# A decode layer on one core: K0 ahead of the q weights, wo behind V15, spread batch rows with one output store, and a W_down tail in rows 6, 2, 1

## The chip, the cores and the metric

The kernel runs on 1 core of one Trainium2 chip. The metric is the device time of one execution in microseconds (us), median of several executions. One execution was recorded by the hardware profiler; the durations below come from that one. Engines: PE (matmul), PEld (PE's weight loads), DVE (vector), ACT (scalar), POOL (GpSimd), SP (sync, which issues nearly all the loads).

## What is computed

One token for each of 4 sequences, through attention over a window of the cache and a gated FFN, all in bf16:

```python
def _A_ref(x, k_cache, v_cache, wq, wo):      # x: 4 x 1 x 576
    W = min(4096, max(256, Sk // 4))          # Sk = 16384, so W = 4096
    q = (x @ wq).reshape(B, Sq, 32, 128)...
    k = jnp.repeat(k_cache[:, :, Sk - W:, :], 2, axis=1)   # 16 key heads, 32 query heads
    v = jnp.repeat(v_cache[:, :, Sk - W:, :], 2, axis=1)
    p = _softmax(einsum("bhqd,bhkd->bhqk", q, k) * 128 ** -0.5)
    return einsum("bhqk,bhkd->bhqd", p, v)... @ wo
h = x + _A_ref(_layernorm(x), ...)
gate, up = h_norm @ W_gate, h_norm @ W_up     # 576 x 4608 each; h_norm = _layernorm(h)
h2 = h + ((gate * (gate > 0)) * up) @ W_down  # 4608 x 576
```

So 4 x 16 x 4096 x 128 keys and as many values (67 MB each), and four weight matrices of 4.7 or 5.3 MB, are read once; the arithmetic on them is small.

## The kernel before, in words

**Loads.** SP issues the loads in the order written in the code, one queue, and waits in that order: a load whose place in SBUF is still being read holds up all that come after it. `place` (line 220) keeps for each block of the arena who reads it last, and makes a new load there wait for that reader. `add_kv` (239) loads a tile of 4.19 MB, four key heads of one sequence: K0 to K15 and V0 to V15, into a ring of four slots. The order is wq (4.19 MB, and 0.52 MB more into the buffer pT), K0 to K4, V0, K5, V1, K6, ... K15, V11, V12, V13, V14, wo, V15, then W_gate, W_up, and W_down in four chunks, the last of them in rows 0 to 6 and 6 to 9. With this order wq has slot 3 and K0, K1, K2 have slots 0, 1, 2; K3 takes slot 3 again, K4 slot 0. The weights wo, W_gate, W_up and W_down lie where the q matrices and the four slots were.

**Attention.** A tile K is turned in place by two DVE transposes (`turn_k`, line 420, halves w = 0 and 1; the transpose itself is line 428), then PE multiplies it with q (`pe_qk`, 431; its matmul is line 446): 16 matmuls per half, four per head. `by_head` (31) names the halves that are turned in a second layout, in which PE reads the keys with another stride: in the profile the transpose takes about 7.3 us instead of 4.4, a matmul 0.227 us instead of 0.43 at full clock. Before the change these are the second halves of K0, K2, K3 and K4. Scores of four tiles (one sequence) gather in PSUM; `row_max` (451), `head_max` (456) and `exps` (464) make the exponentials, eight ACT operations; `turn_p` (477) turns them with two DVE transposes; `pe_pv` (483) multiplies with V; `select_o`, `weights` and `finish_o` reduce to the output of a sequence. `do_k` and `do_v` (561, 587) write the order out by hand. For g = 4 the row max, one head of QK(4,0), the head max and the exponentials of sequence 0 come ahead of the transpose of K4's second half.

**Start.** POOL builds constants (291 to 339), among them a memset of 6.9 us over the q area (299). ACT loads x (348), DVE takes its statistics (350) and normalizes; PE turns x (`pe_x`), DVE stores it (`dve_x`, 396 to 402); then c_am and c_msk, two DVE operations on a POOL constant (538, 540). `pe_q` (379) multiplies with wq, ACT evicts (`act_q`), 32 small matmuls turn q (QT), DVE stores it (`dve_q`, "qkeep", line 405), ACT spreads it into the block matrices (`put_q`, 412, "QW").

**End.** WO (622), layer norm by matmuls with ones, the FFN (GU, 668, gate first, then up), its product (HH, 675), transposes (681), DOWN (701): 144 matmuls of 144 columns, four column groups n in four partition groups of 32. DVE evicts [128, 144] (704). The four batch rows lie in partitions 32n to 32n+3, and four stores write them, two from SP and two from ACT (706 to 708).

Of the kernel before, what the change touches and what calls it, by code (L numbers as in the profile page):

```python
# [11 lines left out]
B = 4  # L12
D = 576
# [17 lines left out]
def by_head(g, w):  # L31
    return (g, w) in ((0, 1), (2, 1), (3, 1), (4, 1))

# [87 lines left out]
def bass_sequential_preLN__sliding_block_cached__glu_gated_reglu__decode_kernel(  # L121
# [12 lines left out]
    with ExitStack() as es:  # L134
        cnt = [0]

        def sb(name, shape, dt):
            return es.enter_context(nc.sbuf_tensor("sb_" + name, shape, dt))
# [54 lines left out]
        tmp5 = sb("tmp5", [128, DC, B], FP32)  # L193
        out_sb = sb("out_sb", [128, 144], BF16)


# [36 lines left out]
        def ring_slot():  # L233
            s = ring[0] % NSLOT
            ring[0] += 1
            return s
# [15 lines left out]
        def last_rows(W):  # L252
            return W[512:576, :].rearrange("r (a n) -> (r a) n", a=2)

        s = ring_slot()
        wq_off = slot0 + s * TILE
        place(("wq", 0), wq_off, TILE, "QMM",
              lambda e: e.dma_start(out=arena[:, wq_off:wq_off + TILE], in_=main_rows(A_wq)), key=f"slot{s}")
        P.dma("sync", ("L", "wq", 1), lambda e: e.dma_start(out=pT[:, 0:2048], in_=last_rows(A_wq)), "d_wq1")
        for g in range(NTILE):  # L260
            add_kv("K", g)
            if g >= 4:
                add_kv("V", g - 4)
# [3 lines left out]
        for g in range(NTILE - 4, NTILE):  # L267
            if g == NTILE - 1:
                place(("wo",), WO_OFF, H * D, "WO",
                      lambda e: e.dma_start(out=arena[:, WO_OFF:WO_OFF + H * D], in_=A_wo.rearrange("(p r) n -> p (r n)", p=128)))  # L270
            add_kv("V", g)
        gu_off = {}
        off = WO_OFF + H * D
# [20 lines left out]

        pool("c_xnT", lambda e: e.memset(xnT[:, :, :], 0.0))
        pool("c_m40", lambda e: e.memset(c_m4[:, :, :], 0.0))
# [3 lines left out]
        pool("c_idf0", lambda e: e.memset(ident_f[:, :], 0.0))  # L300
        pool("c_idf", lambda e: e.affine_select(out=ident_f[:, :], in_=ident_f[:, :], pattern=[[-1, 128]],
                                                compare_op=ALU.not_equal, fill=1.0, base=0, channel_multiplier=1), ["c_idf0"])
        pool("c_am0", lambda e: e.memset(c_am[:, :, :, :], 0.0))
# [39 lines left out]
        dve("c_par", lambda e: e.tensor_scalar(out=par[:, 1:2], in0=par[:, 0:1], scalar1=-1.0, scalar2=1.0,  # L343
                                               op0=ALU.mult, op1=ALU.add), ["c_par0"])


# [17 lines left out]
        def chunk(t, td, c):  # L364
            return td if c == 4 else t[:, 0:512].rearrange("b (p r) -> b r p", r=4)[:, c, :]
# [161 lines left out]
        def finish_o(b):  # L527
# [9 lines left out]
        dve_x()  # L537
        dve("c_am", lambda e: e.tensor_reduce(out=am[:, :], in_=c_am[:, :, :, :].rearrange("p a m s -> p a (m s)"), axis=AX.X, op=ALU.max),
            ["c_am1"])
        dve("c_msk", lambda e: e.tensor_scalar(out=msk[:, :], in0=am[:, :], scalar1=-1.0, scalar2=BIG, op0=ALU.add, op1=ALU.mult), ["c_am"])  # L540
        pe_q()
# [5 lines left out]
        dve("c_e8", lambda e: e.tensor_reduce(out=e8[:, :], in_=c_e8[:, :, :], axis=AX.X, op=ALU.max), ["c_e81"])  # L547
        dve("c_sel", lambda e: e.tensor_reduce(out=sel4[:, 0:4], in_=c_s4[:, :, :], axis=AX.X, op=ALU.max),
            ["c_s41", "c_sel0"])
        for q in range(4):  # L550
            dve("c_selc", lambda e, q=q: e.tensor_copy(out=selc[:, q, :, q], in_=e8[:, :]), ["c_e8", "c_selc0"])
        turn_k(0, 0)
        turn_k(0, 1)

        late = []

        def flush():
            while late:
                late.pop(0)()

        def do_k(g):
            b, qd = divmod(g, 4)
            if g:
                turn_k(g, 0)
            if g == 5:
                turn_p(0, 0)
                turn_p(0, 1)
            flush()
            if g == 4:
                row_max(0)  # L570
                pe_qk(g, 0, range(1))
                head_max(0)
                exps(0)
                turn_k(g, 1)
                pe_qk(g, 0, range(1, 4))
                put_q(2)
            else:
                if g:
                    turn_k(g, 1)
# [50 lines left out]
        for c in range(DC):  # L630
            pe("HT", lambda e, c=c: e.matmul(m_ps[:, c * 4:(c + 1) * 4], lhsT=chunk(part, partd, c), rhs=sel4[:, 0:4],
                                             start=True, stop=True), ["part0", "part1", "partd", "c_sel"] if c == 0 else [])
# [18 lines left out]
        dve("n2a", lambda e: e.tensor_tensor(out=tmp5[:, :, :], in0=tmp5[:, :, :], in1=rstd_bc, op=ALU.mult), ["n1", "s6"])  # L651
        dve("n2", lambda e: e.tensor_copy(out=hnT[:, 0:4, 0:4], in_=tmp5[:, 0:4, :]), ["n2a", "c_hnT"])
        for a in range(2):
            dve("n3", lambda e, a=a: e.tensor_scalar(out=hnT[:, 4 + a, 0:4], in0=tmp5[:, 4, :], scalar1=par[:, a:a + 1], scalar2=None,
                                                     op0=ALU.mult), ["n2a", "c_hnT"])
# [32 lines left out]
        for n in range(4):  # L688
            pe(None, lambda e, n=n: e.matmul(bank[0][32 * n:32 * n + 32, 0:144], lhsT=sel4[:, :], rhs=part[:, 144 * n:144 * (n + 1)],
                                             start=True, stop=False, skip_group_check=True), [("G", 0)])  # L690
        for n in range(4):
            pe(None, lambda e, n=n: e.matmul(bank[0][32 * n:32 * n + 32, 0:144], lhsT=ident_b[0:B, 0:32], rhs=x_bf[:, 144 * n:144 * (n + 1)],
                                             start=False, stop=False, skip_group_check=True))
        for j in range(4):
            wv = arena[:, wd_off[j]:wd_off[j] + WDJ].rearrange("p (r n) -> p r n", n=D)
            for r in range(9):
                for n in range(4):
                    deps = []
                    if n == 0 and (r == 0 or (j == 3 and r == 6)):
                        deps = [("L", "wd", j, r)] + (["HC0", "HC1", "HC2"] if j == 0 else [])  # L700
                    pe("DOWN", lambda e, j=j, r=r, n=n, wv=wv: e.matmul(  # L701
                        bank[0][32 * n:32 * n + 32, 0:144], lhsT=hhT[:, r * 128 + 32 * j:r * 128 + 32 * j + 32],
                        rhs=wv[:, r, 144 * n:144 * (n + 1)], start=False, stop=(j == 3 and r == 8), skip_group_check=True), deps)
        dve("OUT", lambda e: e.tensor_copy(out=out_sb[:, :], in_=bank[0][:, 0:144]), ["DOWN"])
        orow = out.rearrange("b s d -> (b s) d")
        for n in range(4):
            P.dma("sync" if n % 2 == 0 else "scalar", ("O", n),
                  lambda e, n=n: e.dma_start(out=orow[:, 144 * n:144 * (n + 1)], in_=out_sb[32 * n:32 * n + 4, :]), f"d_out{n}", ["OUT"])
        P.op("sync", None, None, [("O", n) for n in range(4)])
        P.emit(nc, es)  # L710
# [28 lines left out]
```

## Time and profile before

| | us |
|---|---|
| median of 3 runs | 383.94 (383.39 to 384.01) |
| the profiled execution, its own time | 384.01 |
| its span (first to last event on the core) | 382.2 |
| PE, DVE, ACT, POOL busy | 281.2, 222.0, 37.5, 16.1 |
| bytes moved in the span | 159.81 MB, mean 418 GB/s |
| queue of SP's loads, share of the 16 DMA engines' span | 97.5% |
| transposes of K (line 428), 32 | 152.8 in all |
| matmuls with K (line 446), 512 | 212.6 in all |

The page's slices show the rates along the span, each slice 9.55 us; a digit is a share in tenths, PEclk the clock granted to PE:

```profile
PEclk9967999987999897898998987989998956558667
DMA  8999999998999999999999999999999999999993
GB/s 330 439 439 434 429 429 429 422 434 336 432 424 415 433 439 435 432 436 434 425 425 429 434 439 432 427 429 436 425 430 436 439 427 433 421 450 422 420 406 143
```

Busy times overlap, so they don't add up to the span. In rows of the timeline the columns are start, busy time, engine, line, operation, out<-in, count, and in brackets the idle time ahead of it and who ended it. SPq is SP issuing a load.

### The profile page before, as it was taken

How to read it: one execution, taken by the hardware profiler on the slowest of the kernel's cores; microseconds unless marked ns; L12 is line 12 of the kernel's file. 1: busy time of each engine (PE TensorE's matmuls, PEld its weight loads, DVE VectorE, ACT ScalarE, POOL GpSimd, SP SyncE). 2: the span in 40 equal slices, each digit the busy share in tenths (PEclk: the TensorE clock that was granted, in tenths of full speed). 3: DMA queues.
4: the chain of work that ended last, by engine and by line, in shares of the span. 5: the costliest groups of instructions: out<-in, count | busy, mean ns of one | idle time of the engine just before them, and what ended most of it. 6: DMA issues, size and time to landing. Idle time of an engine off the chain costs nothing.

```text
span 382.2 us, 3671 instructions
## 1 busy us (share of the span) xinstructions
PE 281.2 (74%) x1629; PEld 92.1 (24%) x1629; DVE 222.0 (58%) x157; ACT 37.5 (10%) x95; POOL 16.1 (4%) x38
## 2 busy tenths in 40 slices
PE   0509999969989792979996948889969537036654
PEld 0202223313222221322221212222212213015322
DVE  4159999789484918965737369766464455102111
ACT  3120000070000006100000041000000340000100
POOL 8700000000000000000000000000000000000000
PEclk9967999987999897898998987989998956558667
DMA  8999999998999999999999999999999999999993
GB/s 330 439 439 434 429 429 429 422 434 336 432 424 415 433 439 435 432 436 434 425 425 429 434 439 432 427 429 436 425 430 436 439 427 433 421 450 422 420 406 143
DMA packets 6390, 159.81 MB, mean 418 GB/s; under 512 B 740, under 2 KB 744, under 8 KB 1384
## 3 DMA queue, kind: packets, MB, share of 16 engines
q1 hardware_dynamic: 6352, 159.59, 97.5%
q8 instruction: 12, 0.20, 0.2%
q14 instruction: 2, 0.02, 0.0%
q10 hardware_dynamic: 24, 0.01, 0.0%
HBM read 159.58 MB, written 0.00 MB: 418 GB/s over the span
## 4 chain that ended last, share of the span: by engine, by line
PE 47%; DMA 34%; DVE 15%; ACT 2%; SPq 1%; issue 1%
PE psb L446 40%; DMA sb_arena<-in_A_k_cache_dram 19%; DVE sb_arena L428 12%; DMA sb_arena<-in_B_W_down_dram 9%; DMA sb_arena<-in_A_v_cache_dram 7%; PE psb L493 5%; ACT sb_pp L471 2%; DVE sb_o_sel L505 1%; DVE sb_o_tmp L501 1%; DVE sb_pp L480 1%; PE psb L465 0%; PE psb L530 0%; SPq L285 0%; DVE sb_gm L459 0%; DVE sb_gm L461 0%
## 5 line engine op out<-in xcount | busy, mean ns | idle before, releaser
L446 PE MATMUL psb<-sb_arena 128*128 128x512 bf16 x512 | 212.6, 585 | 22.2 <-DVE sb_arena L428 22.1
L428 DVE STREAM_TRANSPOSE sb_arena<-sb_arena 128x4096 f32<-128x4096 f32 x32 | 152.8, 4804 | 48.0 <-DMA sb_arena<-in_A_k_cache_dram 48.0
L446 PEld LDWEIGHTS psb<-sb_arena 128*128 128x128 bf16 x512 | 56.6, 113 | 169.6 <-issue 134.9
L493 PE MATMUL psb<-sb_arena,sb_pp 128*32 128x512 bf16 x512 | 36.0, 433 | 22.5 <-DMA sb_arena<-in_A_v_cache_dram 15.9
L471 ACT ACTIVATE sb_pp<-psb,sb_stat 128x512 bf16<-128x512 f32 x32 | 24.9, 845 | 259.6 <-DVE sb_stat L466 259.6
L501 DVE TENSOR_TENSOR sb_o_tmp<-psb,sb_qm 128x512 f32<-128x512 f32 x16 | 10.8, 676 | 27.0 <-PE psb L493 26.9
L493 PEld LDWEIGHTS psb<-sb_arena,sb_pp 128*32 128x32 bf16 x512 | 13.6, 106 | 47.6 <-issue 23.0
L453 DVE TENSOR_REDUCE sb_stat<-psb 128x1 f32<-128x1024 f32 x4 | 4.9, 1224 | 26.7 <-PE psb L446 26.7
L480 DVE STREAM_TRANSPOSE sb_pp<-sb_pp 128x2048 bf16<-128x2048 bf16 x8 | 18.0, 2278 | 1.4 <-ACT sb_pp L471 1.4
L505 DVE TENSOR_REDUCE sb_o_sel<-sb_o_tmp 128x128 f32<-128x512 f32 x16 | 16.6, 1036 | 0.5
L530 PE MATMUL psb<-sb_o_sel,sb_selw 128*32 128x32 f32 x128 | 2.2, 221 | 16.3 <-DVE sb_o_sel L505 16.3
L668 PE MATMUL psb<-sb_arena,sb_hnT 128*32 128x384 bf16 x120 | 9.0, 483 | 6.6 <-DMA sb_arena<-in_B_W_up_dram 4.5
L675 DVE TENSOR_TENSOR sb_pp<-psb,sb_pp 128x384 bf16<-128x384 f32 x3 | 1.5, 551 | 13.7 <-PE psb L668 13.7
L371 PE MATMUL psb<-sb_ident_b,sb_xn_bf 4*128 4x4 bf16 x4 | 0.3, 174 | 9.9 <-DVE sb_xnd_bf L360 9.9
L668 PEld LDWEIGHTS psb<-sb_arena,sb_hnT 128*32 128x32 bf16 x120 | 4.4, 135 | 10.6 <-DMA sb_arena<-in_B_W_up_dram 4.9
L299 POOL MEMSET sb_arena<- 128x8192 f32 x1 | 6.9, 6925 | 0.0
L513 PE MATMUL psb<-sb_stat,sb_sameh 128*128 128x1 f32 x8 | 1.7, 286 | 6.7 <-DVE sb_stat L511 6.7
L471 ACT ACTIVATION_READ_ACCUMULATOR sb_pp<-psb,sb_stat 128x1 f32 x32 | 6.5, 204 | 0.0
L530 PEld LDWEIGHTS psb<-sb_o_sel,sb_selw 128*32 128x32 f32 x128 | 1.7, 132 | 17.4 <-DVE sb_o_sel L505 17.4
L701 PE MATMUL psb<-sb_arena,sb_pp 128*32 128x144 bf16 x144 | 3.8, 249 | 2.6 <-DMA sb_arena<-in_B_W_down_dram 2.1
L384 PE MATMUL psb<-sb_arena,sb_xnT 128*32 128x512 bf16 x32 | 3.2, 573 | 2.8 <-DMA sb_arena<-in_A_wq_dram 2.8
L414 ACT COPY sb_arena<-sb_q_keep 32x128 bf16<-32x128 bf16 x16 | 4.8, 302 | 1.5 <-DVE sb_q_keep L405 1.4
(123 smaller groups left out, 71.4 us busy)
## 6 DMA issues: line engine op xcount, KB each, us to landing
sb_arena<-in_A_k_cache_dram SPq DMA_DIRECT2D x16, 4096.0 KB, 19.7
sb_arena<-in_A_v_cache_dram SPq DMA_DIRECT2D x16, 4096.0 KB, 24.4
sb_arena<-in_A_wo_dram SPq DMA_DIRECT2D x1, 4608.0 KB, 15.6
sb_arena<-in_B_W_gate_dram SPq DMA_DIRECT2D x1, 4608.0 KB, 30.5
sb_arena<-in_B_W_up_dram SPq DMA_DIRECT2D x1, 4608.0 KB, 41.9
sb_arena<-in_A_wq_dram SPq DMA_DIRECT2D x1, 4096.0 KB, 12.3
sb_arena<-in_B_W_down_dram SPq DMA_DIRECT2D x3, 1296.0 KB, 31.3
sb_arena<-in_B_W_down_dram SPq DMA_DIRECT2D x1, 864.0 KB, 32.9
```

Of the source, the lines that this page charges most:

```text
L299: pool("c_qW", lambda e: e.memset(arena[:, 0:2 * QWW].bitcast(FP32), 0.0))
L414: act(("QW", b), lambda e, i=i: e.copy(out=bass.AP(tensor=arena, offset=32 * i * AW + b % 2 * QWW + 32 * i, ap=[[AW, 32], [128, 4], [514, ...
L428: dve(("TRA", g, w), lambda e: e.transpose(out=dst, in_=src), [("L", "K", g)] if w == 0 else [])
L446: pe(("QK", g, w), lambda e, off=off, steps=steps, wo_=wo_, qd=qd, first=first, last=a == cb == 3: e.matmul(bank[SB[b % 2] + w], lhsT=aren ...
L453: dve(("MAX", b), lambda e: e.tensor_reduce(out=stat[:, b, 0:1], in_=s_ps, axis=AX.X, op=ALU.max, negate=True), [("QK", 4 * b + 3, 1)])
L471: act(("EXP", b, w), lambda e, w=w, a=a: e.activation(out=bass.AP(tensor=pp, offset=4096 + a // 2 * 2048 + w * 1024 + a % 2, ap=[[8192, 12 ...
L480: dve(("PTR", b, w), lambda e: e.transpose(out=dst, in_=src), [("EXP", b, w), ("PV", 4 * b - 1) if b else "QMM"])
L493: pe(("PV", g), lambda e, j=j, tq=tq, k=k: e.matmul(o_ps[32 * j:32 * j + 32, :], lhsT=pT[:, qd * 1024 + tq * 32:][:, 0:32], rhs=v[:, tq * ...
L501: dve(("OS", g), lambda e: e.tensor_tensor(out=o_tmp[:, :].rearrange("p (t d) -> p t d", t=4), in0=o_ps.rearrange("p (t d) -> p t d", t=4) ...
L505: dve(("OSEL", g), lambda e: e.tensor_reduce(out=o_sel[:, qd, :], in_=o_tmp[:, :].rearrange("p (t d) -> p d t", t=4), axis=AX.X, op=ALU.ad ...
L530: pe(("OT", b), lambda e, q=q, qd=qd: e.matmul(ot_ps[32 * qd:32 * qd + 32, 0:32], lhsT=selw[:, qd, 32 * q:32 * q + 32], rhs=o_sel[:, qd, 3 ...
L668: pe(("GU", g, c // 4), lambda e, g=g, m=m, j=j, lo=lo, c=c: e.matmul(bank[3 * g + m][32 * j:32 * j + 32, 0:384], lhsT=hnT[:, c if c < 4 e ...
```

## The change

Five things are edited:

- K0 is loaded first, ahead of wq. So K0 lies in slot 3, wq in slot 0, K3 follows K0 in slot 3 and K4 follows wq. K0's transposes stand on DVE right behind `dve_x`, ahead of qkeep, and K0's first half is by_head too. c_am and c_msk move on DVE to the front, ahead of x's statistics; on POOL the constant ident_f moves ahead of c_m4 and the long memset.
- For g = 4 the second transpose comes ahead of the row max, three heads of QK(4,0) ahead of the head max and the fourth behind it.
- wo is loaded behind V15.
- The batch rows lie 8 partitions apart from the FFN on (partitions 32n + 8b): hnT and sel4 are written with that stride, x is added through a new small selection matrix xsel, made by two POOL operations. One transfer stores the output.
- The last W_down chunk comes in rows 0 to 6, 6 to 8 and 8 to 9, each waited for by itself.

```diff
-    return (g, w) in ((0, 1), (2, 1), (3, 1), (4, 1))
+    return (g, w) in ((0, 0), (0, 1), (2, 1), (3, 1), (4, 1))
...
+        add_kv("K", 0)
         s = ring_slot()
         wq_off = slot0 + s * TILE
...
-        for g in range(NTILE):
+        for g in range(1, NTILE):
             add_kv("K", g)
...
         for g in range(NTILE - 4, NTILE):
-            if g == NTILE - 1:
-                place(("wo",), WO_OFF, H * D, "WO",
-                      lambda e: e.dma_start(out=arena[:, WO_OFF:WO_OFF + H * D], in_=A_wo.rearrange("(p r) n -> p (r n)", p=128)))
             add_kv("V", g)
+        place(("wo",), WO_OFF, H * D, "WO",
+              lambda e: e.dma_start(out=arena[:, WO_OFF:WO_OFF + H * D], in_=A_wo.rearrange("(p r) n -> p (r n)", p=128)))
...
-            for r0, r1 in ((0, 9),) if j < 3 else ((0, 6), (6, 9)):
+            for r0, r1 in ((0, 9),) if j < 3 else ((0, 6), (6, 8), (8, 9)):
...
+        pool("c_xs0", lambda e: e.memset(xsel[:, :], 0.0))
+        pool("c_xs1", lambda e: e.affine_select(out=xsel[:, :], in_=xsel[:, :], pattern=[[-1, 32]], compare_op=ALU.not_equal,
+                                                fill=1.0, base=0, channel_multiplier=8), ["c_xs0"])
...
+        dve("c_am", ...)
+        dve("c_msk", ...)
...
         pe_x()
         dve_x()
-        dve("c_am", ...)
-        dve("c_msk", ...)
+        turn_k(0, 0)
+        turn_k(0, 1)
         pe_q()
         act_q()
         dve_q()
...
-        turn_k(0, 0)
-        turn_k(0, 1)
...
+            if g:
+                turn_k(g, 1)
             if g == 4:
                 row_max(0)
-                pe_qk(g, 0, range(1))
+                pe_qk(g, 0, range(3))
                 head_max(0)
+                pe_qk(g, 0, range(3, 4))
                 exps(0)
-                turn_k(g, 1)
-                pe_qk(g, 0, range(1, 4))
                 put_q(2)
...
-        dve("n2", lambda e: e.tensor_copy(out=hnT[:, 0:4, 0:4], in_=tmp5[:, 0:4, :]), ["n2a", "c_hnT"])
+        dve("n2", lambda e: e.tensor_copy(out=hnT[:, 0:4, 0:32:8], in_=tmp5[:, 0:4, :]), ["n2a", "c_hnT"])
...
-            pe(None, lambda e, n=n: e.matmul(bank[0][32 * n:32 * n + 32, 0:144], lhsT=ident_b[0:B, 0:32], rhs=x_bf[:, 144 * n:144 * (n + 1)],
+            pe(None, lambda e, n=n: e.matmul(bank[0][32 * n:32 * n + 32, 0:144], lhsT=xsel[:, :], rhs=x_bf[:, 144 * n:144 * (n + 1)],
...
-                    if n == 0 and (r == 0 or (j == 3 and r == 6)):
+                    if n == 0 and (r == 0 or (j == 3 and r in (6, 8))):
...
-        for n in range(4):
-            P.dma("sync" if n % 2 == 0 else "scalar", ("O", n),
-                  lambda e, n=n: e.dma_start(out=orow[:, 144 * n:144 * (n + 1)], in_=out_sb[32 * n:32 * n + 4, :]), f"d_out{n}", ["OUT"])
-        P.op("sync", None, None, [("O", n) for n in range(4)])
+        P.dma("sync", "O", lambda e: e.dma_start(
+            out=out.rearrange("b s (n d) -> n (b s) d", n=4), in_=bass.AP(tensor=out_sb, offset=0, ap=[[8 * 144, 16], [1, 144]])),
+            "d_out", ["OUT"])
+        P.op("sync", None, None, ["O"])
```

More of the change, by code (lines that the diff above doesn't have):

```diff
@@ L194, in bass_sequential_preLN__sliding_block_cached__glu_gated_reglu__decode_kernel @@
         out_sb = sb("out_sb", [128, 144], BF16)
+        xsel = sb("xsel", [B, 32], BF16)
         pT = pp[:, 0:4096]
@@ L295, in bass_sequential_preLN__sliding_block_cached__glu_gated_reglu__decode_kernel @@
         pool("c_xnT", lambda e: e.memset(xnT[:, :, :], 0.0))
+        pool("c_idf0", lambda e: e.memset(ident_f[:, :], 0.0))
+        pool("c_idf", lambda e: e.affine_select(out=ident_f[:, :], in_=ident_f[:, :], pattern=[[-1, 128]],
+                                                compare_op=ALU.not_equal, fill=1.0, base=0, channel_multiplier=1), ["c_idf0"])
         pool("c_m40", lambda e: e.memset(c_m4[:, :, :], 0.0))
@@ L299, in bass_sequential_preLN__sliding_block_cached__glu_gated_reglu__decode_kernel @@
         pool("c_qW", lambda e: e.memset(arena[:, 0:2 * QWW].bitcast(FP32), 0.0))
-        pool("c_idf0", lambda e: e.memset(ident_f[:, :], 0.0))
-        pool("c_idf", lambda e: e.affine_select(out=ident_f[:, :], in_=ident_f[:, :], pattern=[[-1, 128]],
-                                                compare_op=ALU.not_equal, fill=1.0, base=0, channel_multiplier=1), ["c_idf0"])
         pool("c_am0", lambda e: e.memset(c_am[:, :, :, :], 0.0))
@@ L344, in bass_sequential_preLN__sliding_block_cached__glu_gated_reglu__decode_kernel @@
                                                op0=ALU.mult, op1=ALU.add), ["c_par0"])
+        dve("c_am", lambda e: e.tensor_reduce(out=am[:, :], in_=c_am[:, :, :, :].rearrange("p a m s -> p a (m s)"), axis=AX.X, op=ALU.max),
+            ["c_am1"])
+        dve("c_msk", lambda e: e.tensor_scalar(out=msk[:, :], in0=am[:, :], scalar1=-1.0, scalar2=BIG, op0=ALU.add, op1=ALU.mult), ["c_am"])
         act("warm_sqrt", lambda e: e.activation(out=warm[:, 0:1], in_=eps_c[:, :], func=ACT.Sqrt), ["c_eps"])
@@ L537, in bass_sequential_preLN__sliding_block_cached__glu_gated_reglu__decode_kernel @@
         dve_x()
-        dve("c_am", lambda e: e.tensor_reduce(out=am[:, :], in_=c_am[:, :, :, :].rearrange("p a m s -> p a (m s)"), axis=AX.X, op=ALU.max),
-            ["c_am1"])
-        dve("c_msk", lambda e: e.tensor_scalar(out=msk[:, :], in0=am[:, :], scalar1=-1.0, scalar2=BIG, op0=ALU.add, op1=ALU.mult), ["c_am"])
+        turn_k(0, 0)
+        turn_k(0, 1)
         pe_q()
@@ L547, in bass_sequential_preLN__sliding_block_cached__glu_gated_reglu__decode_kernel @@
         dve("c_e8", lambda e: e.tensor_reduce(out=e8[:, :], in_=c_e8[:, :, :], axis=AX.X, op=ALU.max), ["c_e81"])
-        dve("c_sel", lambda e: e.tensor_reduce(out=sel4[:, 0:4], in_=c_s4[:, :, :], axis=AX.X, op=ALU.max),
+        dve("c_sel", lambda e: e.tensor_reduce(out=sel4[:, 0:32:8], in_=c_s4[:, :, :], axis=AX.X, op=ALU.max),
             ["c_s41", "c_sel0"])
@@ L568, in do_k @@
             flush()
+            if g:
+                turn_k(g, 1)
             if g == 4:
                 row_max(0)
-                pe_qk(g, 0, range(1))
+                pe_qk(g, 0, range(3))
                 head_max(0)
+                pe_qk(g, 0, range(3, 4))
                 exps(0)
-                turn_k(g, 1)
-                pe_qk(g, 0, range(1, 4))
                 put_q(2)
             else:
-                if g:
-                    turn_k(g, 1)
                 pe_qk(g, 0)
@@ L630, in bass_sequential_preLN__sliding_block_cached__glu_gated_reglu__decode_kernel @@
         for c in range(DC):
-            pe("HT", lambda e, c=c: e.matmul(m_ps[:, c * 4:(c + 1) * 4], lhsT=chunk(part, partd, c), rhs=sel4[:, 0:4],
+            pe("HT", lambda e, c=c: e.matmul(m_ps[:, c * 4:(c + 1) * 4], lhsT=chunk(part, partd, c), rhs=sel4[:, 0:32:8],
                                              start=True, stop=True), ["part0", "part1", "partd", "c_sel"] if c == 0 else [])
@@ L651, in bass_sequential_preLN__sliding_block_cached__glu_gated_reglu__decode_kernel @@
         dve("n2a", lambda e: e.tensor_tensor(out=tmp5[:, :, :], in0=tmp5[:, :, :], in1=rstd_bc, op=ALU.mult), ["n1", "s6"])
-        dve("n2", lambda e: e.tensor_copy(out=hnT[:, 0:4, 0:4], in_=tmp5[:, 0:4, :]), ["n2a", "c_hnT"])
+        dve("n2", lambda e: e.tensor_copy(out=hnT[:, 0:4, 0:32:8], in_=tmp5[:, 0:4, :]), ["n2a", "c_hnT"])
         for a in range(2):
-            dve("n3", lambda e, a=a: e.tensor_scalar(out=hnT[:, 4 + a, 0:4], in0=tmp5[:, 4, :], scalar1=par[:, a:a + 1], scalar2=None,
+            dve("n3", lambda e, a=a: e.tensor_scalar(out=hnT[:, 4 + a, 0:32:8], in0=tmp5[:, 4, :], scalar1=par[:, a:a + 1], scalar2=None,
                                                      op0=ALU.mult), ["n2a", "c_hnT"])
@@ L689, in bass_sequential_preLN__sliding_block_cached__glu_gated_reglu__decode_kernel @@
             pe(None, lambda e, n=n: e.matmul(bank[0][32 * n:32 * n + 32, 0:144], lhsT=sel4[:, :], rhs=part[:, 144 * n:144 * (n + 1)],
-                                             start=True, stop=False, skip_group_check=True), [("G", 0)])
+                                             start=True, stop=False, skip_group_check=True), [("G", 0), "c_xs1"])
         for n in range(4):
-            pe(None, lambda e, n=n: e.matmul(bank[0][32 * n:32 * n + 32, 0:144], lhsT=ident_b[0:B, 0:32], rhs=x_bf[:, 144 * n:144 * (n + 1)],
+            pe(None, lambda e, n=n: e.matmul(bank[0][32 * n:32 * n + 32, 0:144], lhsT=xsel[:, :], rhs=x_bf[:, 144 * n:144 * (n + 1)],
                                              start=False, stop=False, skip_group_check=True))
@@ L704, in bass_sequential_preLN__sliding_block_cached__glu_gated_reglu__decode_kernel @@
         dve("OUT", lambda e: e.tensor_copy(out=out_sb[:, :], in_=bank[0][:, 0:144]), ["DOWN"])
-        orow = out.rearrange("b s d -> (b s) d")
-        for n in range(4):
-            P.dma("sync" if n % 2 == 0 else "scalar", ("O", n),
-                  lambda e, n=n: e.dma_start(out=orow[:, 144 * n:144 * (n + 1)], in_=out_sb[32 * n:32 * n + 4, :]), f"d_out{n}", ["OUT"])
-        P.op("sync", None, None, [("O", n) for n in range(4)])
+        P.dma("sync", "O", lambda e: e.dma_start(
+            out=out.rearrange("b s (n d) -> n (b s) d", n=4), in_=bass.AP(tensor=out_sb, offset=0, ap=[[8 * 144, 16], [1, 144]])),
+            "d_out", ["OUT"])
+        P.op("sync", None, None, ["O"])
         P.emit(nc, es)
```

## The prediction, made before the changed kernel had run

> **What bounds the kernel now.** I read the page's span and the table by stage first: how much the DMA engines move in each stretch (last column GB/s, the one before it their busy share).
>
> ```profile
> 0.00:30.00 30.00, 6.56 (x86) 3.12 (x87) 12.67 (x27) 6.76 (x15) 16.09 (x38) 0.88 0.96 402
> 30.00:60.00 30.00, 29.13 (x77) 7.98 (x75) 29.60 (x6) 0.00 (x0) 0.00 (x0) 0.95 1.01 434
> 60.00:84.00 24.00, 22.55 (x71) 7.06 (x69) 20.18 (x8) 5.85 (x15) 0.00 (x0) 1.00 1.00 428
> 84.00:104.00 20.00, 18.48 (x73) 5.63 (x74) 14.43 (x5) 1.51 (x6) 0.00 (x0) 0.83 0.92 383
> 104.00:300.00 196.00, 166.92 (x753) 48.03 (x754) 123.89 (x72) 13.55 (x36) 0.00 (x0) 0.92 1.00 430
> 300.00:360.00 60.00, 26.71 (x342) 14.37 (x334) 18.67 (x37) 8.35 (x20) 0.00 (x0) 0.63 1.01 431
> ```
>
> From 30 us on the stream of loads runs at 428 to 434 GB/s with busy DMA engines, whatever PE and DVE do; I call 431 its full rate. One stretch is short: 84 to 104 us, with 383. So the time is the bytes (159.6 MB; at 431 they take 370 us) plus what the stream loses at its start, in that hole, and behind its last byte. An edit counts only if it changes one of these three.
>
> The hole, by 2 us windows, then SP's queue with the load that ends it and its neighbour, and PE's and DVE's rows there:
>
> ```profile
> 88.00:90.00 2.00, 2.00 (x6) 0.72 (x5) 2.00 (x2) 0.00 (x0) 0.00 (x0) 0.50 0.88 377
> 90.00:92.00 2.00, 2.00 (x7) 0.67 (x6) 2.00 (x2) 0.00 (x0) 0.00 (x0) 0.79 0.46 197
> 92.00:94.00 2.00, 2.00 (x6) 0.57 (x5) 2.00 (x1) 0.00 (x0) 0.00 (x0) 1.00 0.77 246
> ```
>
> ```profile
> 74.89 0.53 SPq L246 DMA_DIRECT2D sb_arena<-in_A_v_cache_dram  x1
> 91.79 0.54 SPq L246 DMA_DIRECT2D sb_arena<-in_A_k_cache_dram  x1
> ```
>
> ```profile
> 78.03 11.69 DVE L428 STREAM_TRANSPOSE sb_arena<-sb_arena 128x4096 f32<-128x4096 f32 x2
> 85.52 13.14 PE L446 MATMUL psb<-sb_arena 128*128 128x512 bf16 x32 [2.33 <-DVE sb_arena L428]
> ```
>
> K6 goes into K4's slot, so SP holds it until QK(4,1), the first 16 of the 32 matmuls at 85.52, is done; these wait for the slow transpose that DVE began at 78.03, behind the softmax steps. V1 had been issued at 74.89, and nothing stood behind it.
>
> **How a late issue becomes lost time.** Up to V1, 4.72 + 8 x 4.19 = 38.27 MB were issued. By 30 us 12.06 MB had moved (30 x 402), so at 431 GB/s the rest lasts until 90.8. K6 came 1.0 us later, and the hole costs 20 x (431-383)/431 = 2.2 us; lines through the cumulated bytes before and after it lie 2.5 us apart. I take **2.4**. So loss = (issue - dry) + 1.4; the 1.4 is what a new transfer needs to get going (first bytes show after 93.0).
>
> **Old hole: -2.4.** In the new order transpose (4,1) follows (4,0), which ended at 72.4 (44.82 + 27.57); the slow form takes 7.25 from start to start (11.69 less the 4.4 of the next), so it ends at 79.7, not 85.3. PE runs three heads of QK(4,0) ahead of the max and one behind it. With PE 2.1 us late (below), QK(3,1) ends at 74.9 + 2.1 = 77.0, three heads (12 x 0.43) at 82.1, row max is long done, head max 0.4, fourth head 1.7, MB 0.4: 84.6; QK(4,1) takes 16 x 0.227 = 3.6 (the 35.90 row below) and ends at 88.2, or at 91.5 at half clock. The stream then is dry at 90.8 + 1.5 (below) = 92.3, so an issue up to 90.9 costs nothing. Next, V2 waits for PV(0): NB 84.8, eight exps 6.2, the second PTR 2.3, PV 1.9 behind QK(5,0): about 98, against a need of 102.0 - 1.4 = 100.6. The hole closes; from K7 on loads are issued some 5 us ahead, as now (17.39 us from issue to landing where 4.19 MB take 9.7).
>
> **New wait at the front.** K0 now takes slot 3 and wq slot 0, so K3, not K4, waits for QK(0,1), and all later loads queue on SP behind it. Before it only 17.30 MB are issued (wq, K0 to K2): dry at 30 + (17.30 - 12.06)/0.431 = 42.1, loss = issue - 40.7. Before, K4 had that wait, with K3 as a cushion of 9.7 us. When is QK(0,1) done? The rows:
>
> ```profile
> 5.81 0.81 DVE L350 BATCH_NORM_STATS2 sb_bn<-sb_x_bf 4x6 f32<-4x288 bf16 x2 [2.84 <-DMA sb_x_bf<-in_A_x_dram]
> 10.70 0.17 DVE L402 CAST sb_xT<-psb 128x20 f32<-128x20 bf16 x1
> 10.85 0.29 DVE L538 TENSOR_REDUCE sb_am<-sb_c_am 128x4 f32<-128x128 f32 x1
> 18.52 0.68 DVE L405 CAST sb_q_keep<-psb 32x512 bf16<-32x512 f32 x1 [7.07 <-PE psb L390]
> ```
>
> ```profile
> 35.90 3.63 PE L446 MATMUL psb<-sb_arena 128*128 128x512 bf16 x16 [0.25 <-DVE sb_arena L428]
> ```
>
> - c_am and c_msk move ahead of the statistics on DVE. c_am needs POOL's c_am1, which still ends at 10.8 (c_idf only changes places with c_m4 and the 6.9 us memset). So the statistics start at 11.45 in place of 5.81, and dve_x ends 5.06 later, at 16.5, not 10.9. K0 is there at 13.1 (as wq was) and waits for DVE.
> - Both transposes of K0 are now the slow form: 16.5 + 2 x 7.25 = 31.0. Queued behind them is qkeep. The q path reaches it by 29.5 at the latest: wq is complete where K0 was, 24.06; 3.6 of matmuls, eviction, 1.1 of QT. So DVE decides.
> - qkeep 0.7, four QW copies 1.3: QK(0,0) starts at 33.1 (28.59 before).
> - 32 matmuls at 0.227 (both halves are by_head now) would end at 40.3. But PE has stood still for some 4 us. In the trace the granted clock fell to half at 22.8, 4.2 us behind PE's last work, and came back 4.0 us after the start at 28.59 and 5.1 after 85.52; at half clock a matmul takes 0.43. Each us at half adds 0.47: with 4.0 us, QK(0,1) ends at **42.2**.
>
> So **K3 is issued at 42.2, loss 1.5** (0 at full clock; 2.0 at 5.1 us). PE begins K1 2.1 us later than now (40.15), the 2.1 used above; K3's transposes (56.4 at the earliest by DVE) meet its landing at 44.8 + 9.7 + 1.5 = 56.0, so nothing is pushed further.
>
> [...]
>
> **wo behind V15: 0.** V15 no longer waits behind wo for PV(12) (314.73), it goes out at about 301; it lands a wo (10.9 us) earlier, near 329, so the W_down loads are issued near 333 and not at 343.68. WO starts at wo's landing, 340, and not at 346.37. But the FFN's end waits for W_up (PE idle 4.5 us until 366.1) and then for W_down, bytes that keep their place. Cover: V15's 9.7 us behind V14. If it were gone, wo's issue would dry the queue, up to 1 us; the other end is 0.
>
> **The end.**
>
> ```profile
> 378.54 0.42 PE L701 MATMUL psb<-sb_arena,sb_pp 128*32 128x144 bf16 x6 [0.15 <-DMA sb_arena<-in_B_W_down_dram]
> 379.12 0.42 PE L701 MATMUL psb<-sb_arena,sb_pp 128*32 128x144 bf16 x6 [0.16 <-issue]
> 379.59 0.31 DVE L704 CAST sb_out_sb<-psb 128x144 bf16<-128x144 f32 x1 [6.19 <-PE psb L701]
> 379.93 0.67 SPq L708 DMA_DIRECT2D out_dram<-sb_out_sb  x2
> ```
>
> - Last chunk 6, 2, 1: 12 matmuls follow the last landing, 378.54 to 379.57. Two rows now land one row's bytes (0.147 MB, 0.34 us) earlier; their 8 matmuls run ahead, 4 stay. **-0.35**. Bounds: -0.7 (8 of the 12) to +0.35 (the third transfer's small pieces cost one row's time again; none of this size is in the trace).
> - One store: SP's two issues take 0.67, the second is gone: **-0.3**, bounds -0.5 and +0.2 (a K load's issue takes 0.54, not 0.33).
> - Spread rows in hnT, sel4 and xsel keep shapes and counts; two POOL operations on xsel run beside the first transposes; eviction has the same 128x144. 0.
>
> **Sum.** The profiled execution took 384.01 (span 382.2, 1.8 around it), the median is 383.94; I count from 384.01: -2.4 + 1.5 - 0.35 - 0.3 = -1.55: **382.5** (381.6 to 383.4 by the bounds on the clock and the end). A measurement here tells about 0.2%, 0.77 us, from no change.
>
> **Rivals.**
> - *No new hole* (0.20): QK(0) runs at full clock, K3 is issued at 40.3, or a new transfer gets going in less than 1.4. For: 32 fast matmuls fit just in time. Against: PE's idle time before them. -2.4 - 0.65: **380.9**.
> - *The front hole decides* (0.13, slower): PE stays at half clock through QK(0), 32 x 0.43 = 13.8, K3 goes out at 46.8 and the stream loses 6.1; 384.01 + 6.1 - 3.05 = **387.0**. It turns to a loss once QK(0,1) ends later than 43.8, and beyond noise from 44.5. For: K3 has no cushion. Against: the clock came back within 5.1 us each time.
> - *The old hole only moves* (0.12): QK(4,1) or PV(0) comes too late again and 1.5 or more of the 2.4 stays: **384.5**, same or a little slower. Against: 2.7 us of room by the rows above.
>
> The forecast has 0.55. Faster by over 0.2%: 0.47 of it and the first rival, 0.67; within: 0.08 and 0.07, 0.15; slower: 0.13 and 0.05, 0.18. The range, 380.5 to 384.9, takes in no new hole with the best end and leaves most of the slower case out.
>
> **What would show it.** Statistics at 11.4; qkeep at 31; QK(0,0) near 33 at half clock; K3's issue near 42 and a dip in GB/s at 42 to 45; none at 90 to 95; K6's issue near 88; four matmuls behind the last landing, one store. Wrong if QK(0,1) ends before 41 or after 44, or K6 after 91.

## The result and the profile after

The changed kernel takes 381.81 us (median of 4 runs, 381.41 to 381.90), the kernel before beside it 383.66; the ratio is 0.9952, with a 95% interval of 0.9934 to 0.9970. So it is faster, by 0.5%; forecast were 382.5, in a range of 380.5 to 384.9. The profiled execution took 381.90 with a span of 379.9 (384.01 and 382.2 before).

The table by stage of the changed kernel, in the same columns as before (the last is GB/s):

```profile
0.00:30.00 30.00, 5.64 (x82) 2.76 (x82) 18.83 (x22) 4.53 (x8) 16.51 (x40) 1.00 0.95 402
30.00:60.00 30.00, 28.80 (x77) 8.80 (x78) 24.17 (x11) 2.24 (x8) 0.00 (x0) 0.89 0.98 419
60.00:84.00 24.00, 23.70 (x75) 7.40 (x74) 21.74 (x8) 0.15 (x1) 0.00 (x0) 1.00 1.01 437
84.00:104.00 20.00, 18.66 (x79) 5.41 (x77) 13.71 (x5) 7.23 (x20) 0.00 (x0) 1.00 1.02 438
104.00:300.00 196.00, 165.76 (x761) 48.69 (x760) 124.35 (x75) 13.56 (x36) 0.00 (x0) 0.90 1.00 431
```

The stretch from 84 to 104 us moves 438 GB/s, not 383: the hole is gone. SP's queue and the rows behind it show why:

```profile
75.67 0.54 SPq L247 DMA_DIRECT2D sb_arena<-in_A_v_cache_dram  x1
87.22 0.54 SPq L247 DMA_DIRECT2D sb_arena<-in_A_k_cache_dram  x1
```

```profile
72.67 7.38 DVE L435 STREAM_TRANSPOSE sb_arena<-sb_arena 128x4096 f32<-128x4096 f32 x1
...
81.43 1.88 PE L453 MATMUL psb<-sb_arena 128*128 128x512 bf16 x4
83.24 0.38 PE L472 MATMUL psb<-sb_scl,sb_gm 1*128 1x1 f32 x2
83.55 3.63 PE L453 MATMUL psb<-sb_arena 128*128 128x512 bf16 x16
```

K4's second half is turned before the softmax steps, so its 16 matmuls start at 83.55 and not at 85.52, run at full clock (1.00 from 84 to 104 us), and K6 goes out at 87.2 (91.8 before). Of these 4.6 us the earlier start is 2.0 and the clock 2.6: before, the granted clock was 0.50 until 90.8, and the 16 matmuls took 6.2 us where they now take 3.6. By an estimate from these rows, the old start at full clock (85.52 + 3.63 = 89.2) would just have met the 89.4 (90.8 - 1.4) up to which K6 can go out without a loss; no run has the old order at full clock. The front came out earlier than forecast:

```profile
11.18 0.80 DVE L357 BATCH_NORM_STATS2 sb_bn<-sb_x_bf 4x6 f32<-4x288 bf16 x2
12.76 0.42 DVE L362 TENSOR_SCALAR sb_xn_bf<-sb_x_bf,sb_mv 4x576 bf16<-4x576 bf16 x1
14.51 0.17 DVE L409 CAST sb_xT<-psb 128x20 f32<-128x20 bf16 x1
29.12 0.65 DVE L412 CAST sb_q_keep<-psb 32x512 bf16<-32x512 f32 x1
```

The statistics do wait for POOL's constants (11.18), but from there to the end of dve_x it takes 3.5 us, not 5.06; qkeep comes at 29.1 (forecast 31.0), QK(0,0) at 31.2 (33.1). The granted clock (the column ahead of the DMA share, 0.52 from 35 to 37) stays at half until nearly 37, and SP issues K3, with K4 right behind it, at 41.12 (forecast 42.2):

```profile
35.00:37.00 2.00, 2.00 (x6) 0.72 (x5) 2.00 (x1) 0.00 (x0) 0.00 (x0) 0.52 0.92 385
```

```profile
41.12 1.18 SPq L247 DMA_DIRECT2D sb_arena<-in_A_k_cache_dram  x2
```

**A measure for all runs.** Cumulating the bytes by windows of 1 us and laying a line of 431 GB/s from zero beside them gives by how many us the stream runs late at each place; what the span has beyond that lag near its end is time that the stream doesn't explain. "Late" is a mean over the stretch.

| kernel | late at 20-38 | at 60-88 | at 200-300 | span | span less late | median | ratio to before, interval |
|---|---|---|---|---|---|---|---|
| before | 2.0 | 2.0 | 4.3 | 382.2 | 377.9 | 383.66 | |
| changed | 2.4 | 2.4 | 2.4 | 379.9 | 377.5 | 381.81 | 0.9952 (0.9934 to 0.9970) |
| order_alone | 2.0 | 1.9 | 2.0 | 379.1 | 377.1 | 381.27 | 0.9944 (0.9928 to 0.9961) |
| no_order | 2.4 | 2.5 | 4.0 | 381.7 | 377.7 | 383.76 | 1.0007 (0.9992 to 1.0022) |
| old_front | 2.0 | 1.9 | 1.9 | 379.4 | 377.5 | 381.50 | 0.9951 (0.9932 to 0.9969) |
| late_stats | 2.5 | 8.6 | 8.5 | 386.1 | 377.6 | 387.05 | 1.0101 (1.0078 to 1.0125) |
| wo_first | 2.4 | 2.6 | 2.7 | 379.7 | 377.0 | 381.83 | 0.9962 (0.9950 to 0.9975) |
| two_pieces | 2.4 | 2.6 | 2.7 | 379.8 | 377.1 | 381.97 | 0.9969 (0.9958 to 0.9981) |
| four_stores | 2.4 | 2.6 | 2.6 | 381.2 | 378.6 | 383.11 | 0.9997 (0.9986 to 1.0009) |
| pad_pe | 2.4 | 2.5 | 2.5 | 379.5 | 377.0 | 381.73 | 0.9964 (0.9949 to 0.9980) |
| after_again | 2.5 | 2.4 | 2.3 | 379.6 | 377.3 | 381.85 | 0.9961 (0.9946 to 0.9975) |
| pad_again | 2.3 | 2.4 | 2.4 | 379.7 | 377.3 | 381.57 | 0.9953 (0.9935 to 0.9972) |
| cam_back | 2.3 | 2.8 | 2.8 | 380.2 | 377.4 | 381.97 | 0.9963 (0.9947 to 0.9979) |
| old_front_pad | 2.0 | 1.9 | 2.0 | 378.8 | 376.8 | 380.99 | 0.9933 (0.9915 to 0.9951) |

Before, the stream falls 2.4 us back between 88 and 98 us and never makes it up. In the changed kernel it starts 0.4 later and falls back no more. In the table that is 1.9 us less lag (4.3 to 2.4), and with 0.4 less behind the stream (377.9 to 377.5) it makes the 2.3 us between the spans; the medians lie 1.85 apart. The 0.4 can't be put down to the edits of the end: order_alone, which has the end of the kernel before, shows 377.1, and the kernels with the new end and one store lie between 376.8 and 377.7.

### The profile page after: what moved, and what is told of

Same layout as the page of the kernel before. It is cut to its first block, busy times and chain, and to the rows that moved or that the text cites. A ratio compares the mean times of both kernels' runs of the same rounds, so it can differ in the third digit from the quotient of the medians.

```text
span 379.9 us, 3671 instructions
## 1 busy us (share of the span) xinstructions
PE 279.6 (74%) x1629; PEld 93.6 (25%) x1629; DVE 223.1 (59%) x157; ACT 37.6 (10%) x95; POOL 16.5 (4%) x40
## 4 chain that ended last, share of the span: by engine, by line
PE 44%; DMA 37%; DVE 14%; POOL 2%; issue 1%; ACT 0%; SPq 0%; POOLq 0%
PE psb L453 38%; DMA sb_arena<-in_A_k_cache_dram 18%; DMA sb_arena<-in_B_W_down_dram 11%; DVE sb_arena L435 11%; DMA sb_arena<-in_A_v_cache_dram 8%; PE psb L500 4%; POOL sb_arena L303 2%; DVE sb_o_sel L512 1%; DVE sb_o_tmp L508 1%; PE psb L537 0%; ACT sb_arena L421 0%; SPq L286 0%; PE psb L525 0%; PE psb L520 0%; PE psb L472 0%
## 5 line engine op out<-in xcount | busy, mean ns | idle before, releaser
L453 PE MATMUL psb<-sb_arena 128*128 128x512 bf16 x512 | 209.2, 579 | 10.5 <-DVE sb_arena L435 8.0
L435 DVE STREAM_TRANSPOSE sb_arena<-sb_arena 128x4096 f32<-128x4096 f32 x32 | 156.0, 4898 | 47.6 <-DMA sb_arena<-in_A_k_cache_dram 47.6
L625 PE MATMUL psb<-sb_arena,sb_oT 128*32 128x288 bf16 x64 | 4.0, 445 | 4.9 <-DMA sb_arena<-in_A_wo_dram 4.9
L704 PE MATMUL psb<-sb_arena,sb_pp 128*32 128x144 bf16 x144 | 4.6, 301 | 1.7 <-DMA sb_arena<-in_B_W_down_dram 0.7
## 6 DMA issues: line engine op xcount, KB each, us to landing
sb_arena<-in_B_W_up_dram SPq DMA_DIRECT2D x1, 4608.0 KB, 42.2
```

Source lines behind the costliest of these rows:

```text
L435: dve(("TRA", g, w), lambda e: e.transpose(out=dst, in_=src), [("L", "K", g)] if w == 0 else [])
L453: pe(("QK", g, w), lambda e, off=off, steps=steps, wo_=wo_, qd=qd, first=first, last=a == cb == 3: e.matmul(bank[SB[b % 2] + w], lhsT=aren ...
L704: pe("DOWN", lambda e, j=j, r=r, n=n, wv=wv: e.matmul(bank[0][32 * n:32 * n + 32, 0:144], lhsT=hhT[:, r * 128 + 32 * j:r * 128 + 32 * j + 32],
```

## The experiments

My theory after the result: the new order for g = 4 is the whole gain; the early K0 brings nothing and costs the late start; the edits at the end do little. The rival: the early K0, with its faster matmuls, is what lets PE come in time. Kernels compared below as neighbours ran on one chip, beside the kernel before.

**order_alone**: the kernel before with this edit only.

```diff
+            if g:
+                turn_k(g, 1)
             if g == 4:
                 row_max(0)
-                pe_qk(g, 0, range(1))
+                pe_qk(g, 0, range(3))
                 head_max(0)
+                pe_qk(g, 0, range(3, 4))
                 exps(0)
-                turn_k(g, 1)
-                pe_qk(g, 0, range(1, 4))
```

> The kernel before, with only the new order for g = 4 (second transpose ahead of the row max, three heads ahead of the head max). Theory: the hole at 91 us was the whole gain, and this order alone closes it: QK(3,1) ends at 74.9 as before, (4,1) is turned by 79.7, K6 goes out near 87 (91.8 before, dry at 90.8), GB/s from 84 to 104 near 430, time 2.2 to 2.6 below before, 381.2 to 381.6. Rival: without K0 ahead of wq PE comes too late, K6 still goes out after 90.5 and half or more of the hole stays, time 382.8 or more.

K6 goes out at 86.68, 84 to 104 us move 430 GB/s, 381.27 us. The theory holds, the rival falls: this edit alone takes as much as the whole change.

**no_order**: the changed kernel without that edit (the diff above, reversed).

> The changed kernel, with the old order for g = 4. Theory: the hole is back. QK(3,1) ends at 75.7, the softmax steps and the second transpose follow, QK(4,1) ends near 92.5 at half clock; the stream is dry near 91.2 and loses 2.3 to 2.7 us, time 2.3 to 2.7 above the changed kernel, 384.1 to 384.6. Rival (K0 ahead of wq and its fast layout make the gain by an earlier PE): K6 near 89, time within 0.7 of the changed kernel.

383.76, the time of the kernel before; the windows show the hole again:

```profile
88.00:90.00 2.00, 2.00 (x6) 0.69 (x5) 2.00 (x2) 0.00 (x0) 0.00 (x0) 0.51 0.87 377
90.00:92.00 2.00, 2.00 (x8) 0.63 (x7) 2.00 (x2) 0.00 (x0) 0.00 (x0) 1.00 0.73 311
92.00:94.00 2.00, 2.00 (x6) 0.57 (x5) 2.00 (x2) 0.00 (x0) 0.00 (x0) 1.00 1.03 279
```

The stream falls back by 1.5 us, less than the 2.3 to 2.7 I expected (with its start 2.5 late it is dry at 91.3, and the prediction's law gives 90.98 - 91.3 + 1.4 = 1.1): PE's clock (the column ahead of the DMA share) was back at full near 90, and K6 went out at 90.98, not near 92.5. The direction is settled, the size moved with the clock.

**old_front**: the changed kernel with the old front.

```diff
-        add_kv("K", 0)
         s = ring_slot()
...
-        for g in range(1, NTILE):
+        for g in range(NTILE):
...
         dve_x()
-        turn_k(0, 0)
-        turn_k(0, 1)
+        dve("c_am", ...)
+        dve("c_msk", ...)
```

and `by_head` without (0, 0), K0 turned behind the constants, the constant ident_f back at its place.

> The changed kernel, with the front of the kernel before: wq first, K0 behind it, c_am and c_msk behind dve_x, K0 turned behind the constants, its first half in the old layout. Theory: the front brings nothing and costs the 0.35 us by which the stream starts later; it comes back, the cumulated bytes run 2.0 us and not 2.4 us behind a line of 431 GB/s from zero, no dip at 42, none at 91; time 0.3 to 0.4 below the changed kernel, near 381.4. Rival (the early K0 is needed to close the hole): a dip at 91 of over 1 us, time over 382.5.

Late 2.0 from the start and to the end, no hole; span 379.4 (379.9 with the early K0), 381.50. The ratios, 0.9951 and 0.9952, don't tell the two apart; the lag does. Four kernels with wq first run 2.0 us late, all with K0 first 2.3 to 2.5. Of the difference SP's issue explains a part: 0.65 us for a K tile where wq took 0.42. In the first 4 us 132 GB/s moved, 214 before.

**late_stats**: the changed kernel, in which x's statistics wait for POOL, so that all of the front comes later.

```diff
-                [("L", "x")] if hf == 0 else [])
+                [("L", "x"), "c_toq4"] if hf == 0 else [])
```

> The changed kernel, with the statistics of x held until POOL's fourth selection for toq (near 17.9 us, a wait that nothing in the computation needs). Each step of the front then comes 6.7 us later: dve_x ends at 21.3, K0 is turned by 36, qkeep at 36, QK(0,0) at 38, QK(0,1) ends near 47.8 and K3 goes out there. Theory (the slower rival's mechanism: K3 has no cushion, a late issue costs one for one from a threshold): in the changed kernel K3 went out at 41.1 and lost 0.1, so the threshold is near 41.1 and this one loses 6.6; by the 1.4 of the prediction the threshold lies at 41.1 too, since the stream starts 0.35 later. Time 388.0 to 388.8. Rival (the four loads behind K3 or the later slack give it back): under 385.

SP issues K3 at 47.29, and the DMA engines stand still before it:

```profile
40.00:42.00 2.00, 2.00 (x7) 0.63 (x5) 2.00 (x2) 0.00 (x0) 0.00 (x0) 0.50 1.17 500
42.00:44.00 2.00, 2.00 (x9) 0.81 (x8) 2.00 (x1) 0.00 (x0) 0.00 (x0) 0.81 0.09 33
44.00:46.00 2.00, 2.00 (x11) 0.86 (x9) 2.00 (x2) 0.00 (x0) 0.00 (x0) 1.00 0.00 0
46.00:48.00 2.00, 2.00 (x9) 0.74 (x8) 2.00 (x1) 0.00 (x0) 0.00 (x0) 1.00 0.00 0
48.00:50.00 2.00, 2.00 (x6) 0.52 (x5) 2.00 (x1) 0.00 (x0) 0.00 (x0) 1.00 0.94 262
```

The stream loses 6.1 us (2.5 to 8.6) and gives none back in 330 us. With K3's dry time at 17.30 MB / 0.431 + 2.5 = 42.6 and the prediction's 1.4 the threshold is 41.2, and 47.29 - 41.2 = 6.1: the law holds here (in no_order it was 0.4 short). The median, 387.05, is under the 388.0 to 388.8 expected: K3 went out 0.5 earlier than I had worked out, and the profiled execution (388.08) was the longest of the four. The loss that the slower rival of the prediction names is thus real, though here a late front and not half clock through all of QK(0) brings it, and the changed kernel, with K3 at 41.1, stands on its edge.

**wo_first**: the changed kernel with wo issued ahead of V15.

```diff
         for g in range(NTILE - 4, NTILE):
+            if g == NTILE - 1:
+                place(("wo",), ...)
             add_kv("V", g)
-        place(("wo",), ...)
```

> The changed kernel with wo ahead of V15 again. Theory (the move is worth nothing, its cover isn't needed): up to V14 134.9 MB are issued, at 431 GB/s with the 2.4 us of the start the stream is dry near 315.3; wo goes out near 312.6, 2.7 us ahead, more than the 1.4 that a new transfer needs, so no dip at 312 to 320 and the same time within 0.3. The W_down loads then go out at 341 and not at 332, and the long issues of the last two pieces (3.57 and 4.81 us in the changed kernel) are gone without effect. Rival (V15 covers wo): a dip of 0.5 us or more near 315 and the time up by as much.

No dip (421 and 441 GB/s from 312 to 316 and 316 to 320, with wo issued at 312.68), no lag gained there beyond 0.1 (2.6 us at 290 to 300, 2.7 at 330 to 340), 381.83 (0.9962, beside 0.9952 and 0.9961 for the changed kernel). The move brings nothing that shows, and wo needs no cover. The long issues are gone as well: here the last five W_down loads take SP 3.10 us, in the changed kernel 9.74, with no effect on the time.

**two_pieces**: the changed kernel with the last W_down chunk in rows 6 and 3.

```diff
-            for r0, r1 in ((0, 9),) if j < 3 else ((0, 6), (6, 8), (8, 9)):
+            for r0, r1 in ((0, 9),) if j < 3 else ((0, 6), (6, 9)):
...
-                    if n == 0 and (r == 0 or (j == 3 and r in (6, 8))):
+                    if n == 0 and (r == 0 or (j == 3 and r == 6)):
```

> The changed kernel with the last W_down chunk in rows 6 and 3 again. Prediction's term: 0.35 us slower, since 12 matmuls follow the last landing and not 4. Theory now: the split brings at most 0.1, because in the changed kernel PE stops 0.6 us among the last 12 matmuls without a landing that ends it (377.05 against the landing near 376.4); here the last 12 begin near 376.4 and end within 0.6 to 1.2, the time is within 0.3 of the changed kernel, above or below.

Span less late is 377.1 with two pieces, 376.8 to 377.7 in the kernels with three and one store; the time is 0.1 above that of wo_first beside it, inside the intervals. The third piece brings nothing that shows.

**four_stores**: the changed kernel with four stores, from the spread rows.

```diff
-        P.dma("sync", "O", ...)
...
+        for n in range(4):
+            P.dma("sync" if n % 2 == 0 else "scalar", ("O", n),
+                  lambda e, n=n: e.dma_start(out=orow[:, 144 * n:144 * (n + 1)],
+                      in_=bass.AP(tensor=out_sb, offset=32 * n * 144, ap=[[8 * 144, 4], [1, 144]])), f"d_out{n}", ["OUT"])
...
```

> The changed kernel with four stores of four rows, two from SP and two from ACT, from the spread rows. Prediction's term: 0.3 us slower. Theory now: the one store takes SP 0.68 us to issue, two small ones took 0.67, so from the eviction's end to the span's end it is 2.2 to 2.3 us (2.17 with one store) and the time is up by 0.1 at most.

Wrong: 383.11, some 1.2 us above its neighbours, and the place is plain. The stores' issue in this kernel, and in the changed one:

```profile
377.87 1.49 SPq L711 DMA_DIRECT2D out_dram<-sb_out_sb  x2
377.88 1.33 ACTq L711 DMA_DIRECT2D out_dram<-sb_out_sb  x2
```

```profile
377.73 0.68 SPq L708 DMA_DIRECT2D out_dram<-sb_out_sb  x1
```

A store of four rows took 0.33 us to issue in the kernel before, where the rows lie in adjacent partitions; from rows 8 partitions apart it takes 0.75, and one store of all 16 takes 0.68. From the issue to the span's end it is 3.3 us here, 2.17 in the changed kernel, 2.27 before. So spread rows with four stores would cost 1.1 us; with one store they come out 0.1 ahead of adjacent rows with four.

**pad_pe**: the changed kernel with 40 small matmuls behind the transposes of x. In the changed kernel PE stops among its last 12 matmuls, and no landing ends the stop:

```profile
376.15 0.30 PE L704 MATMUL psb<-sb_arena,sb_pp 128*32 128x144 bf16 x5 [0.18 <-DMA sb_arena<-in_B_W_down_dram]
377.05 0.30 PE L704 MATMUL psb<-sb_arena,sb_pp 128*32 128x144 bf16 x7 [0.60 <-issue]
```

```diff
         pe_x()
+        for c in range(40):
+            pe(None, lambda e: e.matmul(bank[3][0:32, 400:404], lhsT=ident_b[:, 0:32], rhs=ident_b[:, 0:4], start=True, stop=True))
         dve_x()
```

> The changed kernel with 40 small matmuls (4 columns, into a PSUM corner that nobody reads) behind the transposes of x, in a time in which PE has nothing to do. They shift every later place of PE's instruction stream by 80 instructions. Theory (the stop of 0.6 us ahead of PE's last 6 or 7 matmuls is a fetch of instructions that ends late; it stands at the same count from the end with and without the third piece): the stop leaves the last 12 matmuls and falls into a wait for W_down, the last matmul comes 0.4 to 0.6 us earlier, the time is 0.4 to 0.6 below the changed kernel, near 381.3. Rival (the stop is the wait for the last piece): it stays, no change in time.

The weight loads of pad_pe's last 12 matmuls now split 8 and 4, where the code waits for the last row, and a landing ends that wait:

```profile
376.35 0.12 PEld L706 LDWEIGHTS psb<-sb_arena,sb_pp 128*32 128x32 bf16 x8 [0.39 <-DMA sb_arena<-in_B_W_down_dram]
376.66 0.10 PEld L706 LDWEIGHTS psb<-sb_arena,sb_pp 128*32 128x32 bf16 x4 [0.19 <-DMA sb_arena<-in_B_W_down_dram]
```

Eviction begins 1.36 us after the six rows' matmuls do, 2.00 in the changed kernel: the stop is gone though the last piece is still waited for, so it isn't the wait for the last piece. That it is a fetch of instructions, as the theory has it, no profile shows. The time, 381.73, doesn't show it.

**after_again** and **pad_again**: the same two kernels beside each other.

> The changed kernel again, beside the others on one chip: K3's issue near 41.1, no hole at 42 or 91, a stop of 0.5 to 0.9 us among PE's last 12 matmuls; ratio to the kernel before 0.995 to 0.997.

> The changed kernel with the 40 small matmuls once more, beside the changed kernel on one chip: the stop is gone in the profile, eviction begins 1.3 to 1.5 us after the landing of the six rows (2.0 with the stop), time 0.3 to 0.6 below the changed kernel; if the stop is in this profile alone and not in most executions, less than 0.2.

381.85 (ratio 0.9961) and 381.57 (0.9953). In after_again's profile the stop was only 0.3 us, so padding had little to remove there; the intervals overlap. The stop is absent in all three profiles with padding (the third is old_front_pad). Of the eleven without, nine have a break of about 0.3 us or more behind the sixth of PE's last 12 weight loads, cam_back one of 0.1 and order_alone none, so padding is not the only thing that it varies with. A gain in time is not shown.

**cam_back**: the changed kernel with c_am and c_msk behind K0's transposes.

```diff
-        dve("c_am", ...)
-        dve("c_msk", ...)
...
         turn_k(0, 0)
         turn_k(0, 1)
+        dve("c_am", ...)
+        dve("c_msk", ...)
```

> The changed kernel with c_am and c_msk behind K0's transposes on DVE, so x's statistics come when x lands (5.8) and not behind POOL's constants (11.2). Theory on the size of the step: the normalization of x took 2.04 us in the kernel before because POOL's 6.9 us memset ran beside it, and 0.42 in the changed kernel behind the memset; here it runs beside the memset again, 1.8 to 2.2 us. dve_x then ends near 10.9, K0 is turned from its landing (12.6 to 13.1) to 27.6, and now the q path decides (qkeep near 29), so K3's issue stays near 41 and the time within 0.2 of the changed kernel. By the prediction's chain (DVE decides) QK(0,0) would start 1.6 us earlier. Rival for the size: 0.42 here too, then its cause lies elsewhere.

x's statistics came at 3.5, and then, on DVE and on POOL:

```profile
5.06 4.98 DVE L359 TENSOR_SCALAR sb_xn_bf<-sb_x_bf,sb_mv 4x576 bf16<-4x576 bf16 x1
```

```profile
2.81 6.92 POOL L303 MEMSET sb_arena<- 128x8192 f32 x1
```

The normalization took 4.98 us: it ended at 10.04, 0.31 behind the memset's end (9.73). Before, it began at 7.40 and took 2.04, to 9.44, again 0.31 behind the memset's end (9.13); behind the memset, in the changed kernel, it took 0.42. The cause is as I thought, the size (1.8 to 2.2) was not: by these rows it isn't slowed, it waits. K3 went out at 39.75 and qkeep at 29.24, when the q path was through, as expected; the time, 381.97, is that of after_again. The stream lost 0.5 us at 42 to 46 all the same, with K3 earlier than in the changed kernel (which lost 0.0 to 0.1). Small losses of this kind (0 to 0.5 in the kernels with the early K0) don't follow K3's issue; their cause stays open.

**old_front_pad**: old_front with the same 40 matmuls, behind the transposes of q.

> The kernel old_front (the changed kernel with the front of the one before) with the 40 small matmuls behind the transposes of q. Theory: it adds up what held so far: no hole at 91 (order), a stream that starts 0.35 us earlier (front), and no stop among PE's last 12 matmuls (shifted instruction stream): span near 378.8 (old_front 379.4), time 380.7 to 381.1, the lowest here. Rival (nothing left to gain at the end): the time of old_front, 381.5.

380.99, ratio 0.9933 (0.9915 to 0.9951), span 378.8, as expected: the lowest here. Its interval overlaps those of old_front and order_alone, so the last tenths are not settled; that it beats the kernel before is.

## Why the prediction was right, step by step

- *Old hole, -2.4.* Right. The stream regained 2.4 us, K6 went out at 87.2 (forecast 88.2), V2 at 97.5 (98). order_alone and no_order show that this edit alone closes the hole and that the others don't close it without it. Part of the margin was the clock, full throughout QK(4,1); the prediction had allowed for half clock there too, with K6 at 91.5.
- *New wait at the front, +1.5.* The mechanism was right (late_stats), the term too large: 0.0 to 0.1 in the changed kernel. Three sizes were off. The 5.06 us from the statistics to the end of dve_x, taken from the kernel before, held 1.6 us of waiting for POOL's memset, which the move of c_am itself leaves behind; so QK(0,0) came 1.9 us earlier than I had it. The half clock lasted longer: 5.7 us behind the start, not 4.0 (the windows of the kernel before put its returns at 4.2 and 5.3 us, where I had read 4.0 and 5.1), and it came though PE had stood still for 2.3 us and not 4. That took 0.8 of the 1.9 back: 31.2 + 7.26 + 0.47 x 5.7 = 41.1 for K3, 1.1 before the 42.2 forecast. And the stream starts 0.4 later, so it is dry later: the threshold was 41.1, not 40.7, and K3 just met it. These errors don't have one cause, so that K3 went out right at the threshold is luck. The dip forecast for 42 to 45 us does show (279 GB/s from 42 to 44), but 508 GB/s follow from 44 to 46 and the mean lag is 2.4 us on both sides.
- *Front, not priced.* I had the swap of K0 and wq at nothing for the stream; it costs 0.4 us from the first bytes on, gone again in old_front and order_alone.
- *wo behind V15, 0.* Right (wo_first); the loads of W_down went out at 332 (forecast 333), without effect.
- *Last chunk, -0.35.* Not seen: in the changed kernel a stop of PE ahead of its last 7 matmuls takes the place of the 8 that no longer follow the last landing, and two_pieces shows no difference.
- *One store, -0.3.* About -0.1, by one profile of each: one store of 16 spread rows takes as long to issue (0.68) as two of four adjacent rows (0.67).
- *Spread rows, 0.* Right for the arithmetic; for a store it isn't (four_stores), and only the single store covers it.

In sum, the forecast was -2.4 + 1.5 - 0.65 = -1.55. The low end of its bounds, 381.6, agrees with a loss of 1.2 at the front (384.01 - 2.4 + 1.2 - 0.7 - 0.5); no run shows that loss: the kernels with the early K0 lost 0 to 0.5 there, late_stats 6.1. Measured were -1.85 by the medians and -2.3 by the spans of the two profiles: -2.4 for the hole, +0.4 for the start, 0.0 to 0.1 for K3 and -0.4 behind the stream, but for rounding. So the front was put 1.1 us too high, and that the end's 0.65 came is not shown. That forecast and result still lie only 0.7 us apart is due in part to errors of opposite sign. What the rival "no new hole" named is what happened, but by neither of its conditions: PE ran at half clock, and late_stats agrees with the 1.4. The front came earlier and the stream was dry later.

## What to carry to other kernels

When one stream of loads sets the time, price an edit by one question: when does it let each load go out, against the time at which the queue is dry. Past a threshold a late issue cost one for one here, within 0.4 us (6.1 us lost for 6.1 in late_stats, 1.5 for 1.1 in no_order), and nothing downstream gave it back (8.6 us late, then 8.5, in late_stats); before it the stream lost at most 0.5 us, in no order with the issue. Put the operation that frees a load's place ahead of everything that only computes, and take a duration from a stage only after asking what ran beside it there.

## What was not expected of the hardware

- The normalization of x, a DVE tensor_scalar on bf16, took 4.98 us (cam_back) and 2.04 (before) where it began beside POOL's memset of 6.92 us, and ended 0.31 us behind the memset's end both times; behind the memset it took 0.42 (changed kernel). By these three rows it waits for the memset's end, while DVE's statistics don't: 0.80 us beside the memset in cam_back, 0.80 behind it in the changed kernel.
- PE's stop among its last 12 matmuls (0.60 us in the changed kernel) is absent in the three profiles with 80 instructions put ahead of it, and the instruction queue then moved 13 packets of 16 KB, not 12. order_alone, without padding, moved 13 too and has no such stop; cam_back moved 12 and has next to none (0.1 us). What PE stops for is not shown.
- The same four rows cost 0.33 us to issue as a store from adjacent partitions (before) and 0.75 from partitions 8 apart (four_stores).
